# Retention state decayed ahead on GpSimd, and pending conversion work handed out behind the next scores

## Chip, core and metric

The kernel runs on one core of a Trainium2 chip. Its time is the device time of one execution in microseconds (us), the median over several runs. Lower is better. The engines are TensorE (PE; its weight loads are PEld), VectorE (DVE), ScalarE (ACT), GpSimd (POOL) and SyncE (SP, which issues most transfers).

## The reference, cut to what matters

A retention layer feeds two feed-forward layers. There are 2 batches, 8 heads, 768 tokens and a head width of 64; the 1536 token rows have 512 columns.

```python
for t in range(S):                               # retention, per batch and head
    state = gamma * state + outer(k[t], v[t])    # 64 x 64, gamma depends on the head
    y[t] = scale * q[t] @ state
h = x @ w_in;  g = softplus(h);  x = g @ w_out                  # layer 1, d_ff 2048
xn = x / rms(x) * rms_g
out = (silu(xn @ w_gate) * (xn @ w_val)) @ w_out2               # layer 2, d_ff 1536
```

The weights arrive as 64-bit floats; the kernel converts them itself.

## The kernel before, in words

**Tiling.** Retention goes in 12 chunks of 128 tokens (6 per batch; chunk g, place c = g % 6 in its batch). Four chunks make one block of 512 token rows, and there are three blocks. Inside a chunk the recurrence is a matrix product under a causal mask, plus a product with the state carried from the chunk before; one chunk needs these steps:

- `step_t` (L270) turns q and k of a chunk on TensorE (L261). ScalarE copies the turned k (L268), VectorE multiplies the turned q by a table of decays (L263).
- `step_s` (L274) makes the scores of a chunk on TensorE (L280); VectorE multiplies them by two masks (L282), which is what the outputs read.
- `step_y` (L303) makes the outputs on TensorE (L316 from the state, L323 from the masked scores). `split` (L121) takes each of the two halves out of PSUM: ScalarE rounds it to a high part (L122), VectorE subtracts that for a low part (L123). The results are the block's `x`.
- `step_u` (L284) makes the chunk's own contribution `u` to the state on TensorE (L293). VectorE forms the new state as old state times decay plus `u`: a plain copy for c = 0 (L297), four instructions of 64 columns, one per pair of heads, for c = 1 to 4 (L300), nothing for c = 5. The state alternates between two tiles.
- `prep` (L248) scales v on GpSimd (L250).

**Precision.** The large products use three terms: high times high, high times low, low times high. A weight is therefore converted into a high and a low half.

**Conversion of a weight** is in three parts. `convert` (L156) starts it: ScalarE L165 and L166, VectorE L167 and L169, GpSimd L171. It leaves `finish` (L179) in a list of deferred work: VectorE L180. `finish` leaves `last` (L175) there: ScalarE copies the high half (L122) and GpSimd subtracts for the low half (L123). `flush` (L202) runs what is in the list at that moment and then may issue one more weight load on SP (L140). The activation of layer 1 leaves its own split in the same list (`split_later`, L344: ScalarE L122, VectorE L123).

**Order.** The order of instructions is written out by hand: each engine works through its own queue in program order. Chunks 0 to 3 come alone (the loop at L550). Chunks 4 to 11 are each put beside one projection of layer 1, `l1` (L351), 12 matrix products of 512 columns (L340): the loop at L577, with o = 0 to 3 the place in the block and b the block whose layer-1 work runs. There the order of one step is: turn the next chunk, project, then the activation (`after`, L355: ScalarE L357 to L359, VectorE L360), `flush`, outputs, state, next scores, `flush`, `convert`. At chunk 7 the turning of chunk 9 stands between the last scores and the second `flush`. For b = 1, o = 2 and 3, two pieces of layer 1's second product (`l2`, L364, matrix products at L376) follow. Weights are converted in the order `w_in` 0 to 3, then `w_out` 0 to 3: the high half of `w_in` 2 is written in the step of chunk 5, that of `w_in` 3 in chunk 6, `w_out` 0 to 3 in chunks 7 to 10. `l1` of chunk 6 reads `w_in` 2, that of chunk 7 reads `w_in` 3, and the `l2` pieces in the step of chunk 10 read `w_out` 0 to 3. After chunk 11 the rest is layer 1 and layer 2, where TensorE has long runs of products.

The functions around the change:

Of the kernel before, what the change touches and what calls it, by code (L numbers as in the profile page):

```python
# [8 lines left out]
F32 = mybir.dt.float32  # L9
# [3 lines left out]
ALU = mybir.AluOpType  # L13
PSUM = bass.MemoryType.PSUM

P = 128
# [10 lines left out]
def retention_softplus_swiglu(ctx: ExitStack, tc: tile.TileContext, q, k, v, w_in, w_out,  # L27
                              w_gate, w_val, w_out2, rms_g, decay, out):
    nc = tc.nc
    B, H, S, D = q.shape  # L30
# [4 lines left out]
    CPB = S // P  # L35
# [3 lines left out]
    NP = H // 2  # L39
# [3 lines left out]
    const = ctx.enter_context(tc.tile_pool(name="const", bufs=1))  # L43
# [16 lines left out]
    def bank(name):  # L60
        n, s = banks["n"], len(banks["spare"])
        banks["n"] += 1
        if (n + 1) * s // (4 + s) > n * s // (4 + s):
            banks["spare"].append(banks["spare"].pop(0))
            return acc_bank(banks["spare"][-1])
        return ps.tile([P, N], F32, tag="ps", name=name)
# [33 lines left out]
    def load_next(g, weight=False):  # L100
        if g + 1 < NCH:
            load(g + 1, 0)
            load(g + 1, 1)
        if weight:
            load_weight()
        if g < NCH:
            load(g, 2)
# [8 lines left out]
    nc.gpsimd.affine_select(out=causal, in_=causal, pattern=[[1, P]], compare_op=ALU.is_ge,  # L116
                            fill=0.0, base=0, channel_multiplier=-1)
    state = [const.tile([P, NP, D], F32, name=f"state{i}") for i in range(2)]
    nc.scalar.preload_act_table_set("natural_log_exp_and_others")

    def split(hi, lo, src, eng=nc.vector):  # L121
# [18 lines left out]
    def load_weight():  # L140
        i = pos["load"]
        if i >= len(order) or i >= pos["conv"] + STAGE:
            return False
        nm, f = order[i]
        t = stage_p.tile([P, N, 2], U32, tag="stage", name=f"st_{nm}{f}")
        src = srcs[nm]
        if nm in ("w_out", "w_out2"):
            nc.sync.dma_start(out=t, in_=src[f * P:(f + 1) * P])
        else:
            nc.sync.dma_start(out=t.rearrange("p (k f) two -> p k f two", k=KC),  # L150
                              in_=src[:, f * P:(f + 1) * P].rearrange("(k p) f two -> p k f two", p=P))
        staged[i] = t
        pos["load"] += 1
        return True
# [47 lines left out]
    def flush(loads=True):  # L202
        todo = list(deferred)
        deferred.clear()
        for s in todo:
            s()
        if loads:
            load_weight()
# [16 lines left out]
    step = const.tile([P, NP], F32, name="step")  # L225
# [22 lines left out]
    def prep(g):  # L248
        t = qkv[g][2]
        nc.gpsimd.tensor_tensor(out=t, in0=t, in1=dec[:, 1, 0, :, None].to_broadcast([P, H, D]), op=ALU.mult)  # L250
# [19 lines left out]
    def step_t(g, busy=0, order=(1, 0)):  # L270
        turn(g, busy, order)
        turned(g, order)

    def step_s(g):  # L274
        t = tr[g]
        sc = [bank("sc").rearrange("p (j t) -> p j t", j=NP) for _ in range(2)]
        for j in range(NP):
            for e in range(2):
                r = slice(e * D, (e + 1) * D)
                nc.tensor.matmul(sc[e][:, j, :], lhsT=t[r, 1, j, :], rhs=t[r, 0, j, :], start=True, stop=True)  # L280
        for e in range(2):
            nc.vector.tensor_tensor(out=t[:, 2 + e], in0=sc[e], in1=mask[e], op=ALU.mult)  # L282

    def step_u(g):  # L284
        c = g % CPB
        _, kk, vv = [qkv[g].pop(i) for i in range(3)]
        if c == CPB - 1:
            return
        u = bank("u")[:, 0:NP * D].rearrange("p (j t) -> p j t", j=NP)
        for j in range(NP):  # L290
            for e in range(2):
                h = 2 * j + e
                nc.tensor.matmul(u[e * D:(e + 1) * D, j, :], lhsT=kk[:, h, :], rhs=vv[:, NP * e + j, :],  # L293
                                 start=True, stop=True, skip_group_check=True)
        new, old = state[(c + 1) % 2], state[c % 2]
        if c == 0:
            nc.vector.tensor_copy(new, u)  # L297
        else:
            for j in range(NP):
                nc.vector.scalar_tensor_tensor(out=new[:, j], in0=old[:, j], scalar=step[:, j:j + 1], in1=u[:, j],  # L300
                                               op0=ALU.mult, op1=ALU.add)

    def step_y(g):  # L303
        c = g % CPB
# [46 lines left out]
    def l1(b, f):  # L351
        h = bank("h")
        project(h, weight("w_in", f), x[b])

        def after():  # L355
            t = t_p.tile([P, N], F32, tag="t", name="t")
            nc.scalar.activation(out=t, in_=h, func=AF.Abs)  # L357
            nc.scalar.activation(out=t, in_=t, func=AF.Exp, scale=-1.0)
            nc.scalar.activation(out=t, in_=t, func=AF.Ln, bias=1.0)  # L359
            nc.vector.scalar_tensor_tensor(out=t, in0=h, scalar=0.0, in1=t, op0=ALU.max, op1=ALU.add)  # L360
            split_later((b, f), t)
        return after

    def l2(b, gr, m):  # L364
        fs = range(gr * G1, (gr + 1) * G1)
        keep = b == 0
        if keep:
            if gr == 0:
                acc[b, m] = acc_bank(m)
            p = acc[b, m]  # L370
        else:
            p = bank("l2")
        for f in fs:
            w = weight("w_out", f, m == KC - 1)
            for n, (i, j) in enumerate(TERMS):
                nc.tensor.matmul(p, lhsT=w[:, i, m * P:(m + 1) * P], rhs=g_t[b, f][:, j, :],  # L376
                                 start=(n == 0 and f == (0 if keep else fs[0])),
                                 stop=(n == 2 and f == (F1 - 1 if keep else fs[-1])))
        if m == KC - 1:
            for f in fs:  # L380
                g_t.pop((b, f))

        def after():
            if not keep:
                if gr == 0:
                    acc[b, m] = s2_p.tile([P, N], F32, tag="s2", name="x2")
                    nc.scalar.activation(out=acc[b, m], in_=p, func=AF.Copy)
                else:
                    nc.vector.tensor_tensor(out=acc[b, m], in0=p, in1=acc[b, m], op=ALU.add)
            if gr == NG1 - 1:  # L390
                norm(b, m)
        return after
# [134 lines left out]
    def piece(after, conv=1, steps=1):  # L527
        flush()
        for _ in range(conv):
            convert()  # L530
        after()
        if bg:
            step = bg.pop(0)
            if step:
                step()
# [32 lines left out]
    for gr in range(NG1):  # L568
        for b in range(NB):
            l1s = [lambda f=f: l1(b, f) for f in range(gr * G1, (gr + 1) * G1)]  # L570
            if (gr, b) == (NG1 - 1, NB - 1):
                banks["spare"] = list(range(KC))
            l2s = []
            if pend:
                l2s = [lambda m=m: l2(*pend, m) for m in range(KC)]
            if gr == 0 and b < NB - 1:
                for o in range(G1):  # L577
                    g = (b + 1) * CB + o
                    if l2s and o > 1:
                        banks["spare"] = [2, 3] if o == 2 else []  # L580
                    if g + 1 < NCH and g != 2 * CB:
                        step_t(g + 1)
                    after = l1s[o]()
                    if g + 1 < NCH:
                        load_next(g + 2)
                        prep(g + 1)
                    after()
                    flush()
                    step_y(g)
                    step_u(g)  # L590
                    if g + 1 < NCH:
                        step_s(g + 1)
                    if g == 2 * CB - 1:
                        step_t(g + 2)
                    flush()
                    if b == 0 or o < 2:
                        convert()
                    if l2s and o > 1:
                        piece(l2s.pop(0)(), False)
                        piece(l2s.pop(0)(), False)  # L600
            else:
                for n, kind in enumerate("11212122" if (gr, b) == (NG1 - 1, NB - 1) else "12121212"):
                    piece((l1s if kind == "1" else l2s).pop(0)(), n % 2 == 0 and (gr, b) != (NG1 - 1, NB - 1))
            pend = (b, gr)
# [68 lines left out]
```

## Time and profile before

| | us |
|---|---|
| median of 3 timed runs | 627.05 (626.89 to 627.73) |
| profiled execution, span from first to last instruction | 3531.3 |
| PE busy in the profiled execution | 3526.4 |
| DVE, ACT, POOL busy | 360.4, 325.9, 187.2 |

No other time of the profiled execution is given than its span. It lasted 5.63 times as long as the median of the timed runs, and TensorE is busy in nearly all of it. A duration of one instruction is from its start to its written result; when several instructions follow one another on an engine, the distance between their starts (the pitch) is shorter.

### The profile page before, as it was taken

Reading aid. Unit: us, or ns where it says so; the run is one execution under the profiler, and the core shown is the slowest. Engines: PE = TensorE matmul, PEld = TensorE weight load, DVE = VectorE, ACT = ScalarE, POOL = GpSimd, SP = SyncE. Lnnn points to the kernel's source line nnn. Section 1 sums busy time; section 2 is a strip of 40 time slices with the busy share of each in tenths; the row PEclk is TensorE's granted clock in tenths of the full one; section 3 lists DMA queues with packets and bytes.
Section 4 is the critical chain, followed back from the end, with each engine's and each line's share of the span. In section 5 each row is a group of like instructions: output and inputs, shape, how many; then the busy total and the mean of one; then the engine's idle time right before and its main releaser. Section 6 shows DMA issues by size and latency. Waiting matters only on the chain.

```text
span 3531.3 us, 8590 instructions
## 1 busy us (share of the span) xinstructions
PE 3526.4 (100%) x3308; PEld 2460.6 (70%) x3308; DVE 360.4 (10%) x613; ACT 325.9 (9%) x555; POOL 187.2 (5%) x156
## 2 busy tenths in 40 slices
PE   9999999999999999999999999999999999999999
PEld 8777666666666666666776766666666666666666
DVE  1111001101101010011111100000110011100000
ACT  0111011111101010011110010000000000000000
POOL 0001000000000000000000000000000000000000
DMA  3110000000000000000000000000000000000000
GB/s 76 45 33 21 6 12 12 18 18 18 12 0 12 18 18 0 6 18 0 6 18 18 6 18 18 0 12 6 18 18 0 12 10 14 0 0 3 9 6 18
DMA packets 65560, 48.84 MB, mean 14 GB/s; under 512 B 39792, under 2 KB 60528, under 8 KB 65520
## 3 DMA queue, kind: packets, MB, share of 16 engines
q1 hardware_dynamic: 64320, 47.90, 4.6%
q8 instruction: 26, 0.43, 0.0%
q10 hardware_dynamic: 1200, 0.39, 0.0%
q14 instruction: 14, 0.11, 0.0%
HBM read 45.14 MB, written 3.15 MB: 14 GB/s over the span
## 4 chain that ended last, share of the span: by engine, by line
PE 100%; DVE 0%; ACT 0%; issue 0%
PE h L340 19%; PE h_w_val L340 14%; PE h_w_gate L340 14%; PE l L376 12%; PE l L494 10%; PE acc L376 9%; PE acc L494 6%; PE acc L340 6%; PE sc L280 1%; PE y L323 1%; PE pt L261 1%; PE acc L261 1%; PE acc L323 1%; PE acc L280 1%; PE acc L293 1%; PE y L316 0%
## 5 line engine op out<-in xcount | busy, mean ns | idle before, releaser
L340 PE MATMUL h<-x,ws_w_in 128*128 128x512 f32 x516 | 699.5, 1697 | 0.0
L340 PEld LDWEIGHTS h<-x,ws_w_in 128*128 128x128 f32 x516 | 469.4, 911 | 209.0 <-issue 209.0
L340 PE MATMUL h_w_val<-xn,ws_w_val 128*128 128x512 f32 x384 | 519.5, 1693 | 0.0
L340 PE MATMUL h_w_gate<-xn,ws_w_gate 128*128 128x512 f32 x372 | 502.9, 1694 | 0.0
L340 PEld LDWEIGHTS h_w_val<-xn,ws_w_val 128*128 128x128 f32 x384 | 351.1, 916 | 156.0 <-issue 156.0
L340 PEld LDWEIGHTS h_w_gate<-xn,ws_w_gate 128*128 128x128 f32 x372 | 340.1, 914 | 151.8 <-issue 151.4
L376 PE MATMUL l<-g,ws_w_out 128*128 128x512 f32 x324 | 438.4, 1691 | 0.0
L376 PEld LDWEIGHTS l<-g,ws_w_out 128*128 128x128 f32 x324 | 295.3, 912 | 131.7 <-issue 129.2
L494 PE MATMUL l<-ws_w_out,g 128*128 128x512 f32 x261 | 354.6, 1697 | 0.0
L376 PE MATMUL acc<-g,ws_w_out 128*128 128x512 f32 x252 | 340.6, 1699 | 0.0
L494 PEld LDWEIGHTS l<-ws_w_out,g 128*128 128x128 f32 x261 | 236.7, 908 | 106.0 <-issue 104.4
L376 PEld LDWEIGHTS acc<-g,ws_w_out 128*128 128x128 f32 x252 | 229.5, 914 | 102.6 <-issue 100.5
L494 PE MATMUL acc<-ws_w_out,g 128*128 128x512 f32 x171 | 231.1, 1696 | 0.0
L494 PEld LDWEIGHTS acc<-ws_w_out,g 128*128 128x128 f32 x171 | 156.4, 915 | 69.9 <-issue 69.1
L171 POOL TENSOR_TENSOR c<-w,c 128x512 uint32<-128x512 uint32 x68 | 86.0, 1264 | 1635.3 <-DVE w L169 1279.8
L360 DVE SCALAR_TENSOR_TENSOR t<-h,t 128x512 f32<-128x512 f32 x43 | 29.7, 692 | 990.7 <-ACT t L359 990.7
L122 ACT ACTIVATE g<-t 128x512 fp32r<-128x512 f32 x84 | 52.9, 630 | 720.5 <-DVE t L475 686.2
L357 ACT ACTIVATE t<-h 128x512 f32<-128x512 f32 x43 | 25.7, 597 | 1002.7 <-PE h L340 1002.7
L471 ACT ACTIVATE t<-t 128x512 f32<-128x512 f32 x36 | 22.7, 630 | 701.1 <-DVE t L470 701.1
L340 PE MATMUL acc<-x,ws_w_in 128*128 128x512 f32 x60 | 82.6, 1715 | 0.0
L340 PE MATMUL acc<-xn,ws_w_gate 128*128 128x512 f32 x60 | 81.9, 1701 | 0.0
L475 DVE TENSOR_TENSOR t<-h_w_val,t 128x512 f32<-128x512 f32 x32 | 22.1, 691 | 559.3 <-PE h_w_val L340 559.3
(128 smaller groups left out, 1579.8 us busy)
## 6 DMA issues: line engine op xcount, KB each, us to landing
st_w_out<-in_moe_w_out_dram SPq DMA_DIRECT2D x28, 512.0 KB, 3.2
st_w_in<-in_moe_w_in_dram SPq DMA_DIRECT2D x16, 512.0 KB, 3.8
st_w_gate<-in_moe_w_gate_dram SPq DMA_DIRECT2D x12, 512.0 KB, 3.5
st_w_val<-in_moe_w_val_dram SPq DMA_DIRECT2D x12, 512.0 KB, 3.5
v<-in_v_dram SPq DMA_DIRECT2D x12, 256.0 KB, 3.8
q<-in_q_dram SPq DMA_DIRECT2D x23, 128.0 KB, 3.5
k<-in_k_dram SPq DMA_DIRECT2D x23, 128.0 KB, 2.6
out_dram<-o SPq DMA_DIRECT2D x11, 256.0 KB, 2.0
```

The costliest lines, as they stand in the source:

```text
L122: nc.scalar.activation(out=hi, in_=src, func=AF.Copy)
L171: nc.gpsimd.tensor_tensor(out=c, in0=w, in1=c, op=ALU.add)
L261: nc.tensor.transpose(pt[:, j, :], pair(qkv[g][i], j), ident)
L280: nc.tensor.matmul(sc[e][:, j, :], lhsT=t[r, 1, j, :], rhs=t[r, 0, j, :], start=True, stop=True)
L293: nc.tensor.matmul(u[e * D:(e + 1) * D, j, :], lhsT=kk[:, h, :], rhs=vv[:, NP * e + j, :], start=True, stop=True, skip_group_check=True)
L323: nc.tensor.matmul(ys[e][h * D:(h + 1) * D, i, :], lhsT=qkv[g][2][:, NP * e + j, :], rhs=t[:, 2 + e, j, :], start=(c == 0 and i == 0), sto ...
L340: nc.tensor.matmul(h, lhsT=w[:, i, kk * P:(kk + 1) * P], rhs=src[:, j, kk, :], start=(n == 0), stop=(n == 3 * KC - 1))
L357: nc.scalar.activation(out=t, in_=h, func=AF.Abs)
L360: nc.vector.scalar_tensor_tensor(out=t, in0=h, scalar=0.0, in1=t, op0=ALU.max, op1=ALU.add)
L376: nc.tensor.matmul(p, lhsT=w[:, i, m * P:(m + 1) * P], rhs=g_t[b, f][:, j, :], start=(n == 0 and f == (0 if keep else fs[0])), stop=(n == ...
L471: nc.scalar.activation(out=t, in_=t, func=AF.Silu)
L494: nc.tensor.matmul(p, lhsT=g_t[b, f][:, j, m * P:(m + 1) * P], rhs=w[:, i, :], start=(n == 0 and f == (0 if keep else grp[0])), stop=(n == ...
```

## The change

The decayed state is made ahead: after a chunk's state is there, GpSimd multiplies it by the decay into a new tile `faded` (for c = 0 to 3), and the next chunk's state is one VectorE addition of `u` and `faded` over 256 columns instead of four multiply-adds of 64 columns. In the steps of chunks 4 to 11 the first `flush` is moved from ahead of `step_y` to behind `step_s` of the next chunk.

```diff
     state = [const.tile([P, NP, D], F32, name=f"state{i}") for i in range(2)]
+    faded = const.tile([P, NP, D], F32, name="faded")
...
-        new, old = state[(c + 1) % 2], state[c % 2]
+        new = state[(c + 1) % 2]
         if c == 0:
             nc.vector.tensor_copy(new, u)
         else:
-            for j in range(NP):
-                nc.vector.scalar_tensor_tensor(out=new[:, j], in0=old[:, j], scalar=step[:, j:j + 1], in1=u[:, j],
-                                               op0=ALU.mult, op1=ALU.add)
+            nc.vector.tensor_tensor(out=new, in0=u, in1=faded, op=ALU.add)
+        if c < CPB - 2:
+            nc.gpsimd.tensor_tensor(out=faded, in0=new, in1=step[:, :, None].to_broadcast([P, NP, D]), op=ALU.mult)
...
                     after()
-                    flush()
                     step_y(g)
                     step_u(g)
                     if g + 1 < NCH:
                         step_s(g + 1)
+                    flush()
                     if g == 2 * CB - 1:
                         step_t(g + 2)
                     flush()
```

## Rows read from the trace of the kernel before

**Rows 1.** The page: span and busy time of the engines.

```profile
span 3531.3 us, 8590 instructions
PE 3526.4 (100%) x3308; PEld 2460.6 (70%) x3308; DVE 360.4 (10%) x613; ACT 325.9 (9%) x555; POOL 187.2 (5%) x156
```

**Rows 2.** Windows, chunk 4: length, busy PE, PEld, DVE, ACT, POOL, clock, DMA share, GB/s.

```profile
112.89:150.57 37.68, 37.68 (x87) 27.49 (x85) 5.67 (x12) 5.59 (x10) 2.26 (x2) 1.00 0.10 22
```

**Rows 3.** Chain that ended last, the projection of chunk 4: start, length.

```profile
118.26 15.87 PE acc L340 x12
```

**Rows 4.** Timeline of weight loads: first score of chunk 5.

```profile
144.84 0.60 PEld L280 LDWEIGHTS sc<-at 64*128 64x128 f32 x1
```

**Rows 5.** Timeline of ScalarE, chunk 5, and two later rows: start, duration, operation, [idle before].

```profile
171.84 0.60 ACT L357 ACTIVATE t<-acc 128x512 f32<-128x512 f32 x1 [17.83 <-PE acc L340]
174.52 0.63 ACT L122 ACTIVATE g<-t 128x512 fp32r<-128x512 f32 x1 [0.76 <-DVE t L360]
179.90 0.38 ACT L122 ACTIVATE x<-acc 128x256 fp32r<-128x256 f32 x1 [2.17 <-PE acc L323]
180.18 0.62 ACT L122 ACTIVATE ws_w_in<-a 128x512 fp32r<-128x512 f32 x1
180.70 0.66 ACT L165 ACTIVATE c<-st_w_in 128x512 uint32<-128x512 uint32 x1
181.26 0.66 ACT L166 ACTIVATE a<-st_w_in 128x512 f32<-128x512 f32 x1
...
209.44 0.63 ACT L122 ACTIVATE g<-t 128x512 fp32r<-128x512 f32 x1 [0.76 <-DVE t L360]
209.98 0.36 ACT L122 ACTIVATE x<-acc 128x256 fp32r<-128x256 f32 x1
...
260.94 0.60 ACT L268 ACTIVATE at<-pt 128x512 f32<-128x512 f32 x1 [10.80 <-PE pt L261]
261.43 0.62 ACT L122 ACTIVATE ws_w_out<-a 128x512 fp32r<-128x512 f32 x1
```

**Rows 6.** Timeline of VectorE, chunks 4 and 5.

```profile
142.64 0.42 DVE L123 TENSOR_TENSOR x<-acc,x 128x256 fp32r<-128x256 f32 x1 [2.13 <-ACT x L122]
144.96 0.86 DVE L300 SCALAR_TENSOR_TENSOR state<-state,step,u 128x64 f32<-128x64 f32 x4 [1.90 <-PE u L293]
...
173.79 0.69 DVE L360 SCALAR_TENSOR_TENSOR t<-acc,t 128x512 f32<-128x512 f32 x1 [17.13 <-ACT t L359]
174.40 0.68 DVE L180 SCALAR_TENSOR_TENSOR a<-a,c 128x512 f32<-128x512 f32 x1
...
185.60 0.69 DVE L282 TENSOR_TENSOR at<-sc,mask 128x512 f32<-128x512 f32 x1 [4.86 <-PE sc L280]
186.21 0.68 DVE L282 TENSOR_TENSOR at<-acc,mask 128x512 f32<-128x512 f32 x1
186.81 0.42 DVE L167 TENSOR_SCALAR w<-st_w_in 128x512 uint32<-128x512 uint32 x1
187.26 0.69 DVE L169 SCALAR_TENSOR_TENSOR w<-st_w_in,w 128x512 uint32<-128x512 uint32 x1
```

**Rows 7.** Timeline: scaling of v, a weight's low half, and who reads weights first.

```profile
154.39 1.04 POOL L250 TENSOR_TENSOR v<-v,dec 128x512 f32<-128x512 f32 x1
180.88 1.27 POOL L123 TENSOR_TENSOR ws_w_in<-a,ws_w_in 128x512 fp32r<-128x512 f32 x1 [25.45 <-ACT ws_w_in L122]
...
190.08 16.65 PE L340 MATMUL h<-x,ws_w_in 128*128 128x512 f32 x12
...
371.12 32.24 PE L376 MATMUL acc<-g,ws_w_out 128*128 128x512 f32 x24
```

**Rows 8.** Timelines of GpSimd and VectorE later on: two that overlap, and one undisturbed.

```profile
796.62 1.51 POOL L123 TENSOR_TENSOR ws_w_in<-a,ws_w_in 128x512 fp32r<-128x512 f32 x1 [28.27 <-ACT ws_w_in L122]
...
701.81 0.69 DVE L169 SCALAR_TENSOR_TENSOR w<-st_w_in,w 128x512 uint32<-128x512 uint32 x1
...
797.04 1.65 DVE L169 SCALAR_TENSOR_TENSOR w<-st_w_in,w 128x512 uint32<-128x512 uint32 x1
```

## The prediction

> **What bounds the kernel now.** I read the page first [rows 1]. TensorE is busy in 3526.4 of 3531.3 us, VectorE in 360.4, ScalarE in 325.9. But the profiled execution lasted 3531.3 / 627.05 = 5.63 times the median of the timed runs, and nothing but its span is given of what lay around it. So TensorE's durations can't hold in the timed runs: its busy time alone is over five times their length. Those of the other engines can: 360.4 and 325.9 us fit into 627. In the profile everything hides behind a TensorE that is far too slow; the argument has to be made at the timed pace. I take the rows of VectorE, ScalarE and GpSimd as they stand and multiply TensorE's by 627.05 / 3531.3 = 0.178. That is a mean, and an upper one, as the 627.05 also hold waits; the other bound is the row as it stands, where nothing ever waits on another engine and the change is worth nothing.
>
> Next the window of chunk 4 [rows 2]: one retention step beside one projection takes TensorE 37.68 us, at the timed pace 6.69. VectorE is busy 5.67 in it and ScalarE 5.59, so beside a fast TensorE all three are nearly full, and the order of each queue decides who waits. The projection has 15.87 of the 37.68 [rows 3], 2.82 at the timed pace; outputs and state, from its end at 134.13 to the first score at 144.84 [rows 4], 10.71 or 1.90; scores and turning have the rest, 1.97. So from the end of one projection TensorE comes to the next after 1.90 + 1.97 = 3.87 us.
>
> **ScalarE's and VectorE's queues, before.** Count from the start of the activation's first part, just behind the projection. Pitches are taken from ScalarE's rows [rows 5] and VectorE's [rows 6]. VectorE's part of the activation starts at 173.79 - 171.84 = 1.95 us, the split's ScalarE copy at 174.52 - 171.84 = 2.68. Then ScalarE has the two output copies at +0.54 (209.98 - 209.44) and +0.28, taking for the one between two output copies that from an output copy to the weight's copy, 180.18 - 179.90; the weight's high copy starts another 0.28 later, at 3.78, and with 0.62 is done at 4.40. It has waited for nothing: `finish` stood on VectorE right behind the activation. The next projection, for o = 2 and 3, reads that very weight [rows 5, 7]: TensorE is there at 3.87 and waits 0.5 us. Eight of its twelve products need the high half (1.9 us), so the low half, 1.27 us on GpSimd [rows 7], is in time.
>
> **After, part one: the first flush behind the scores.** It removes nothing and adds no instruction. On SP it passes no other transfer: the loads of q, k and v stand ahead of it in both versions, so the weight load keeps its place; on GpSimd `last` keeps its place too. But on VectorE `finish` now stands behind both output splits, the state and both masks, and both flushes run one after the other, so ScalarE meets `last`, which waits for `finish`, at once. VectorE at a pitch of 0.61 for 512 columns (174.40 - 173.79), 0.60 between masks, and 0.34 for 256 columns (0.42 less the 0.08 by which the larger ones' pitch is under their duration) [rows 6]: activation 1.95, splits 2.56 and 2.90, state 3.24, masks 3.58 and 4.18, `finish` 4.78 to 5.46. The weight's copy starts at 5.50 and is done at 6.12, against 4.40. What the move brings forward are the outputs' splits and the masks. Before, VectorE had the activation's split at 175.18 - 171.84 = 3.34, then splits 3.95 and 4.29, state 4.63, masks 5.49 and 6.09 to 6.78; the next outputs begin on TensorE at 6.69, with products that read no mask, so they hardly waited. I take nothing for it.
>
> Twice (`w_in` 2 and 3) a projection on TensorE stands directly behind this copy: 2 x (6.12 - 4.40) = **+3.4 us**. Nothing covers it, as all of TensorE's work up to there is counted in the 3.87.
>
> Behind the waiting copy stand, on ScalarE, the next conversion's two parts (at 6.02 and 6.57), the copy of the next turned k (about 7.1) and the next activation (7.1 + 0.49 = 7.6) [rows 5]. So ScalarE and VectorE form a loop of 7.6 us per step, where TensorE needs 6.69. In the steps of chunks 7, 8 and 9 no projection waits for a weight, and the lateness adds up: 7.1 - 6.7 = 0.4 (at chunk 7 the k copy stands ahead), 0.9, 0.9, together 2.2. In chunk 10's step the `l2` pieces read `w_out` 3 at once [rows 7]: the low half is there at 6.12 + 0.06 + 1.27 + 2.2 = 9.65, before at 4.40 + 0.06 + 1.27 = 5.73, when TensorE came to it with hardly a wait. **+3.9 us**.
>
> **Part two: the state.** Four instructions of 64 columns took 0.86 [rows 6]; one of 256 columns with one input from PSUM takes 0.42 (the split's row [rows 6]). That saves 0.44 in 8 chunks, 3.5 us of VectorE. In steps 4 to 11 it is inside the loop counted above. Chunks 1 to 3 stand alone: VectorE has there two splits 0.7, state 0.86, masks 1.2, turned q 0.6 and a conversion's 1.7, some 5.0 us against TensorE's 3.87, so I take it in full: 3 x 0.44 = **-1.3 us** (bounds 0 and -1.3).
>
> GpSimd's new product of 256 columns has no row. It lies between 0.52, half of v's scaling over 512 columns, and 1.27, the subtraction over 512 [rows 7]; I take 0.55, nearest to the scaling, which is the same operation with a spread factor. GpSimd's step is then 1.04 + 1.26 + 1.27 + 0.55 = 4.1 of 6.7 us, and the result is needed a chunk later: nothing on the path. It waits for the state (about 3.6); behind it in GpSimd's queue stands the weight's low half, which waits for ScalarE until 6.18 anyway. Without that cover it would cost 8 x 0.55 = 4.4.
>
> Two engines can also be in each other's way. While GpSimd subtracted at 796.62, a VectorE instruction with two SBUF inputs took 1.65 us instead of 0.69, and GpSimd's own 1.51 instead of 1.27 [rows 7, 8]. The Trainium skill, "SBUF — State Buffer", section "SBUF: two separate sides", has the rule: the two share a port pair as an exclusive lock, and whoever comes second is blocked for the whole instruction; the trace agrees. By it alone, each new GpSimd product could hold VectorE for its length and the change would be a loss of its own. I take zero: the product starts right after the state, when VectorE does the masks, which have one input from PSUM; no row here shows a mask beside a GpSimd instruction, so this is an argument only. The late weight subtraction (6.2 to 7.5) now meets the next conversion on VectorE, up to 0.96 in six steps; TensorE needs that VectorE work only at about 8.6. Zero, with 5.8 as the end for the range.
>
> **Sum.** 627.05 + 3.4 + 3.9 - 1.3 = 633.05: **633.0 us**.
>
> **Rivals.**
> *VectorE is the bound (faster).* If TensorE's retention work is so short, or the transfers so late, that VectorE sets the pace of all steps, and the weights' copies are not what TensorE waits for, the 8 x 0.44 = 3.5 us come through: 623.5. For it: VectorE's 5.67 of 6.69. Against: the loop of 7.6 is longer than VectorE's own work. It decides where TensorE comes to a projection later than 6.12.
> *TensorE covers all (no change).* If outputs, state, scores and turning take over 6.1 us at the timed pace and not 3.87, the copy is never late: 627 to 627.5. For it: the rows as they stand; the scaling is a mean over two kinds of product, and small ones may scale worse.
> *The lock (slower for another reason).* Eight products of 0.55 blocking VectorE, less the 3.5 saved: a net 0.9, and with the larger clash of 0.96 in six steps up to 5.8 more: 628 to 634. The rule named above would give this. Against it: the masks have one SBUF input.
>
> **Chances.** Forecast 0.50 (629 to 638), lock 0.07, no change 0.20, faster 0.23 (622 to 626). A difference under 0.2%, 1.25 us, can't be told from none. So slower 0.57, same 0.20, faster 0.23. The range reaches from 624.5, which takes in about half of the faster case, to 638, the forecast's upper end with most of the clash; the likeliest case's own range is 629 to 638.
>
> **What would show it.** In the profile of the changed kernel ScalarE's `ws_w_in` and `ws_w_out` copies in chunks 5 to 10 should stand behind an idle stretch that VectorE's L180 ends, and L180 should follow the second mask; if TensorE is as slow there as now, they will, with no cost visible. A VectorE state instruction should take about 0.42, the GpSimd product about 0.55, and the masks should stay at 0.69. The prediction is wrong if the time falls: then the copy is not on TensorE's path, and the price of TensorE's small products is the step to blame.

## The result, and the profile after

| | us |
|---|---|
| changed kernel, median of 4 runs | 634.12 (634.06 to 635.76) |
| kernel before, beside it, median of 4 runs | 626.97 (626.88 to 627.73) |
| ratio | 1.0118, 95% interval 1.0106 to 1.0130 |

The change costs 7.15 us. The profile of before that stands ahead of the prediction is of an execution whose TensorE was over five times too slow, so the kernel before was profiled once more, unchanged, as the first experiment: 626.85 us, span 624.9, TensorE busy for 615.0 of it. "Before" below is that execution (its lines have the numbers used above); the lines of the changed kernel are one higher (L341 for L340, L181 for L180).

The page of the changed kernel: span, busy time, and two groups of matrix products (busy time, mean ns of one | idle before).

```profile
span 632.5 us, 8577 instructions
PE 617.5 (98%) x3308; PEld 511.2 (81%) x3308; DVE 385.4 (61%) x589; ACT 322.2 (51%) x555; POOL 198.7 (31%) x164
...
L341 PE MATMUL h<-x,ws_w_in 128*128 128x512 f32 x516 | 126.0, 394 | 4.7 <-ACT ws_w_in L123 4.7
...
L377 PE MATMUL acc<-g,ws_w_out 128*128 128x512 f32 x252 | 62.4, 398 | 2.1 <-ACT ws_w_out L123 1.5
```

The same lines of before.

```profile
span 624.9 us, 8590 instructions
PE 615.0 (98%) x3308; PEld 510.1 (82%) x3308; DVE 386.7 (62%) x613; ACT 322.0 (52%) x555; POOL 193.3 (31%) x156
...
L340 PE MATMUL h<-x,ws_w_in 128*128 128x512 f32 x516 | 124.5, 390 | 1.6 <-ACT ws_w_in L122 1.6
...
L376 PE MATMUL acc<-g,ws_w_out 128*128 128x512 f32 x252 | 60.8, 391 | 0.5 <-POOL ws_w_out L123 0.5
```

Two things are to be seen. TensorE waits 4.7 us, not 1.6, for the high half of `w_in`, and 2.1, not 0.5, for `w_out`. And the same 516 and 252 products take 1.5 and 1.6 us longer, though none was added. The first is the mechanism of the forecast, the second was not in it.

The wait on its three engines: the timeline of the changed kernel, VectorE's rows of the step of chunk 5, then ScalarE's and TensorE's of this step and the next.

```profile
40.57 0.41 DVE L124 TENSOR_TENSOR x<-acc,x 128x256 fp32r<-128x256 f32 x1
40.91 0.68 DVE L283 TENSOR_TENSOR at<-sc,mask 128x512 f32<-128x512 f32 x1
41.50 0.68 DVE L283 TENSOR_TENSOR at<-acc,mask 128x512 f32<-128x512 f32 x1
42.10 0.68 DVE L181 SCALAR_TENSOR_TENSOR a<-a,c 128x512 f32<-128x512 f32 x1
...
37.68 0.60 ACT L358 ACTIVATE t<-acc 128x512 f32<-128x512 f32 x1 [1.58 <-PE acc L341]
...
42.81 0.63 ACT L123 ACTIVATE ws_w_in<-a 128x512 fp32r<-128x512 f32 x1 [1.82 <-DVE a L181]
...
52.02 0.63 ACT L123 ACTIVATE ws_w_in<-a 128x512 fp32r<-128x512 f32 x1 [2.15 <-DVE a L181]
...
43.50 3.02 PE L341 MATMUL h<-x,ws_w_in 128*128 128x512 f32 x12 [2.12 <-ACT ws_w_in L123]
...
52.70 4.57 PE L341 MATMUL h<-x,ws_w_in 128*128 128x512 f32 x12 [2.58 <-ACT ws_w_in L123]
```

The same copies and projections of before.

```profile
41.85 0.63 ACT L122 ACTIVATE ws_w_in<-a 128x512 fp32r<-128x512 f32 x1 [0.59 <-DVE a L180]
...
49.33 0.63 ACT L122 ACTIVATE ws_w_in<-a 128x512 fp32r<-128x512 f32 x1
...
42.53 3.02 PE L340 MATMUL h<-x,ws_w_in 128*128 128x512 f32 x12 [0.76 <-ACT ws_w_in L122]
...
50.01 3.04 PE L340 MATMUL h<-x,ws_w_in 128*128 128x512 f32 x12 [0.86 <-ACT ws_w_in L122]
```

`finish` (L181) now stands behind both masks, ScalarE stands idle 1.82 and 2.15 us for it, and TensorE 2.12 and 2.58. The second of these projections then takes 4.57 us instead of 3.04.

Windows of 1 us over that projection in the changed kernel: length, busy PE, PEld, DVE, ACT, POOL, granted clock, DMA share, GB/s.

```profile
52.00:53.00 1.00, 0.30 (x1) 0.30 (x2) 0.97 (x3) 0.98 (x2) 0.28 (x1) 0.81 0.90 171
53.00:54.00 1.00, 1.00 (x3) 0.81 (x3) 1.00 (x1) 1.00 (x3) 1.00 (x1) 0.50 0.99 214
...
56.00:57.00 1.00, 1.00 (x6) 0.70 (x4) 0.00 (x0) 0.00 (x0) 1.00 (x2) 0.98 0.77 283
```

The granted clock falls from 1.00 to 0.50, that is from 2.4 to 1.2 GHz, at the end of the wait of 2.58 us. It is 0.50 in the three windows from 53 to 56, and 0.98 in the one from 56. The second place is the last weight of `l2`. TensorE's timeline there in the changed kernel, and a window over the second row, with the fields as above:

```profile
85.78 0.73 PE L377 MATMUL acc<-g,ws_w_out 128*128 128x512 f32 x2 [1.52 <-ACT ws_w_out L123]
87.13 4.65 PE L377 MATMUL acc<-g,ws_w_out 128*128 128x512 f32 x13 [0.62 <-POOL ws_w_out L124]
...
88.00:89.00 1.00, 1.00 (x3) 0.71 (x3) 0.00 (x0) 0.00 (x0) 0.00 (x0) 0.50 0.00 0
```

And before:

```profile
80.99 3.24 PE L376 MATMUL acc<-g,ws_w_out 128*128 128x512 f32 x13 [0.50 <-POOL ws_w_out L123]
```

Thirteen products take 4.65 us behind the waits of 1.52 and 0.62, with the clock at 0.50 again, and 3.24 behind one of 0.50.

ScalarE's first rows of the activations of chunks 7 to 10 in the changed kernel:

```profile
57.30 0.60 ACT L358 ACTIVATE t<-h 128x512 f32<-128x512 f32 x1 [3.04 <-PE h L341]
64.43 0.58 ACT L358 ACTIVATE t<-h 128x512 f32<-128x512 f32 x1
72.02 0.59 ACT L358 ACTIVATE t<-h 128x512 f32<-128x512 f32 x1
79.64 0.59 ACT L358 ACTIVATE t<-acc 128x512 f32<-128x512 f32 x1
```

Those of chunks 7 and 10 before.

```profile
53.09 0.60 ACT L357 ACTIVATE t<-h 128x512 f32<-128x512 f32 x1 [1.51 <-PE h L340]
...
74.40 0.60 ACT L357 ACTIVATE t<-acc 128x512 f32<-128x512 f32 x1 [0.48 <-PE acc L340]
```

**The account**, along the activations and TensorE, spans 632.5 - 624.9 = 7.6 us:

| stretch | after | before | difference |
|---|---|---|---|
| to the first projection | 27.68 | 27.39 | +0.29 |
| from there to the activation of chunk 7 | 29.62 | 25.70 | +3.92 |
| from there to that of chunk 10 | 22.34 | 21.31 | +1.03 |
| from there to the low half of the last `w_out` | 7.49 | 6.59 | +0.90 |
| the 13 products behind it | 4.65 | 3.24 | +1.41 |

The sum is 7.55; what follows is equal. The +3.92 are 3.08 more of waiting for weights and 4.57 - 3.02 = 1.55 of half clock, less 0.61 that before waits for a turned q (TensorE's first scores at 39.59) and after does not, and a rest of -0.1.

### The profile page after: what moved, and what is told of

It reads as the page before. It is cut to its first block, busy times and chain, and to the rows that moved or that the text cites. A ratio compares the mean times of both kernels' runs of the same rounds, so it can differ in the third digit from the quotient of the medians.

```text
span 632.5 us, 8577 instructions
## 1 busy us (share of the span) xinstructions
PE 617.5 (98%) x3308; PEld 511.2 (81%) x3308; DVE 385.4 (61%) x589; ACT 322.2 (51%) x555; POOL 198.7 (31%) x164
## 4 chain that ended last, share of the span: by engine, by line
PE 89%; DVE 3%; ACT 3%; DMA 2%; SPq 1%; issue 1%; POOL 0%; POOLq 0%
PE h L341 18%; PE h_w_val L341 14%; PE h_w_gate L341 13%; PE l L377 12%; PE l L495 9%; PE acc L377 9%; PE acc L495 6%; PE acc L341 6%; DVE at L283 1%; DMA k<-in_k_dram 1%; DMA v<-in_v_dram 1%; DVE x L124 1%; DMA q<-in_q_dram 1%; ACT t L359 1%; ACT t L360 1%; DVE t L361 1%
## 5 line engine op out<-in xcount | busy, mean ns | idle before, releaser
L341 PE MATMUL h<-x,ws_w_in 128*128 128x512 f32 x516 | 126.0, 394 | 4.7 <-ACT ws_w_in L123 4.7
L341 PEld LDWEIGHTS h<-x,ws_w_in 128*128 128x128 f32 x516 | 97.7, 190 | 25.5 <-ACT ws_w_in L123 5.2
L341 PE MATMUL h_w_val<-xn,ws_w_val 128*128 128x512 f32 x384 | 92.3, 389 | 0.0
L341 PE MATMUL h_w_gate<-xn,ws_w_gate 128*128 128x512 f32 x372 | 89.4, 389 | 0.0
L341 PEld LDWEIGHTS h_w_val<-xn,ws_w_val 128*128 128x128 f32 x384 | 72.0, 188 | 14.9
L341 PEld LDWEIGHTS h_w_gate<-xn,ws_w_gate 128*128 128x128 f32 x372 | 69.8, 188 | 14.5
L377 PE MATMUL l<-g,ws_w_out 128*128 128x512 f32 x324 | 78.0, 389 | 0.0
L377 PEld LDWEIGHTS l<-g,ws_w_out 128*128 128x128 f32 x324 | 60.7, 188 | 12.6
L377 PE MATMUL acc<-g,ws_w_out 128*128 128x512 f32 x252 | 62.4, 398 | 2.1 <-ACT ws_w_out L123 1.5
L495 PE MATMUL l<-ws_w_out,g 128*128 128x512 f32 x261 | 63.0, 390 | 0.0
L181 DVE SCALAR_TENSOR_TENSOR a<-a,c 128x512 f32<-128x512 f32 x68 | 58.1, 855 | 3.7 <-POOL c L172 3.7
```

What stands on the lines that cost most here:

```text
L181: nc.vector.scalar_tensor_tensor(out=a, in0=a, scalar=TINY, in1=c.bitcast(F32), op0=ALU.is_ge, op1=ALU.mult)
L341: nc.tensor.matmul(h, lhsT=w[:, i, kk * P:(kk + 1) * P], rhs=src[:, j, kk, :], start=(n == 0), stop=(n == 3 * KC - 1))
L495: nc.tensor.matmul(p, lhsT=g_t[b, f][:, j, m * P:(m + 1) * P], rhs=w[:, i, :], start=(n == 0 and f == (0 if keep else grp[0])), stop=(n == ...
```

## The experiments

All ratios are to the kernel before, run beside each kernel on the same chip (626.84 to 626.99), with 95% intervals.

**The kernel before, unchanged**, for a profile at the pace of the timed runs.

> The kernel before, unchanged, for a profile at the timed pace. Theory (late finish): 627; in the steps of chunks 5 and 6 the weight's high copy on ScalarE follows the output copies with no wait, TensorE waits for it at most 0.9 us each time instead of 2.1 and 2.6, a step lasts 6.9 to 7.0 us throughout, and the half-clock stretches of the changed kernel (52.7 to 56.8 and behind the wait of chunk 10) are absent. If TensorE waits as long in the kernel before, the theory falls.

626.85 us; 0.9998 (0.9988 to 1.0008). It shows what the profile ahead of the prediction could not: VectorE and GpSimd are already in each other's way. Timelines of GpSimd and VectorE, steps of chunks 9 and 5:

```profile
70.05 1.04 POOL L250 TENSOR_TENSOR v<-v,dec 128x512 f32<-128x512 f32 x1
...
70.12 1.52 DVE L180 SCALAR_TENSOR_TENSOR a<-a,c 128x512 f32<-128x512 f32 x1 [0.25 <-POOL c L171]
...
40.30 1.52 DVE L180 SCALAR_TENSOR_TENSOR a<-a,c 128x512 f32<-128x512 f32 x1 [0.25 <-POOL c L171]
```

`finish` waits for GpSimd's product `c` (L171), and as that ends, GpSimd goes on to the scaling of v and holds VectorE's `finish` for 1.52 us instead of 0.68. So it is in the steps of chunks 5, 8 and 10 too: L180 starts at 62.87, 70.12 and 77.40 in those of chunks 8 to 10, a loop of 7.25 and 7.28 us.

**The state alone.**

```diff
-            for j in range(NP):
-                nc.vector.scalar_tensor_tensor(out=new[:, j], in0=old[:, j], scalar=step[:, j:j + 1], in1=u[:, j],
-                                               op0=ALU.mult, op1=ALU.add)
+            nc.vector.tensor_tensor(out=new, in0=u, in1=faded, op=ALU.add)
+        if c < CPB - 2:
+            nc.gpsimd.tensor_tensor(out=faded, in0=new, in1=step[:, :, None].to_broadcast([P, NP, D]), op=ALU.mult)
```

> The state's part alone, the first flush where it was. Theory (late finish): no wait is added, and the first 27 us are set by transfers, so the 0.44 us saved per chunk are worth nothing there: 626 to 627.3, ratio 0.999 to 1.001. Rival (GpSimd's new product blocks VectorE, or is late): 630 or more, with masks or other VectorE rows lengthened beside the product.

627.70 us; 1.0013 (1.0004 to 1.0021), 0.4 above what was expected: no gain, if anything a loss. Up to the first projection TensorE waits for transfers of k (1.7 us), for the scaling of v (0.4) and once for ScalarE (0.2), never for VectorE. So VectorE's saving in chunks 1 to 3 frees nothing: in chunks 1 and 2 the 0.43 us end in a new idle stretch of 0.37 ahead of the masks, which wait for their scores. Later the product stands in GpSimd's queue ahead of a weight that TensorE waits for. Timelines of VectorE (a mask of chunk 2), GpSimd and TensorE in this kernel:

```profile
22.76 0.69 DVE L283 TENSOR_TENSOR at<-sc,mask 128x512 f32<-128x512 f32 x1 [0.37 <-PE acc L281]
...
51.02 0.61 POOL L302 TENSOR_TENSOR faded<-state,step 128x256 f32<-128x256 f32 x1 [3.00 <-DVE state L298]
51.59 1.27 POOL L124 TENSOR_TENSOR ws_w_in<-a,ws_w_in 128x512 fp32r<-128x512 f32 x1
...
50.27 2.11 PE L341 MATMUL h<-x,ws_w_in 128*128 128x512 f32 x8 [0.86 <-ACT ws_w_in L123]
52.92 1.19 PE L341 MATMUL h<-x,ws_w_in 128*128 128x512 f32 x4 [0.54 <-POOL ws_w_in L124]
```

The high half is there at 49.59 + 0.63 = 50.22 (ScalarE's row); the low half could start then, but GpSimd first waits for the state and starts it at 51.59. TensorE runs the eight products of the high half and stands still 0.54 us.

**The move alone.**

```diff
                     after()
-                    flush()
                     step_y(g)
                     step_u(g)
                     if g + 1 < NCH:
                         step_s(g + 1)
+                    flush()
```

> The moved flush alone, the state as before. Theory (late finish): the whole loss is here and a little more, since four state instructions stand in the loop with 0.86 instead of 0.42: five steps of 0.44 more, 634 to 637. Rival (the GpSimd product costs the time): 627.

637.01 us; 1.0163 (1.0149 to 1.0177). The whole loss, and 2.9 us more, is in the move. TensorE's rows:

```profile
43.48 4.61 PE L340 MATMUL h<-x,ws_w_in 128*128 128x512 f32 x12 [2.12 <-ACT ws_w_in L122]
54.28 4.43 PE L340 MATMUL h<-x,ws_w_in 128*128 128x512 f32 x12 [2.58 <-ACT ws_w_in L122]
...
90.36 3.25 PE L376 MATMUL acc<-g,ws_w_out 128*128 128x512 f32 x13 [0.62 <-POOL ws_w_out L123]
```

The waits are those of the changed kernel. With the old state in the loop the activations of chunks 8 to 10 start at 66.31, 74.36 and 82.44, steps of 8.05 and 8.08 where the changed kernel has 7.59 and 7.62: the four small instructions cost 0.46 each time once `finish` stands behind them. So the state's part saves some 2 to 3 us here, and nothing alone.

**`finish` back ahead of the outputs, the split of the activation left behind the scores.**

```diff
                     after()
+                    mine = deferred.pop()
+                    flush(False)
+                    deferred.insert(0, mine)
                     step_y(g)
```

(on the changed kernel)

> As the changed kernel, but the weight's finish is handed out ahead of the outputs again, and only the activation's split and the weight's last part stay behind the scores. Theory (late finish): ScalarE meets last with finish long done, the loop is open, no half-clock stretch: 625 to 627.5, so 7 us or more under the changed kernel. Rival (anything else behind the moved flush, or the GpSimd product): 632 to 634 stays.

626.60 us; 0.9996 (0.9987 to 1.0005). One deferred step put back takes the loss away: TensorE waits 1.2 us for `w_in`'s high halves, and the clock is 1.00 throughout. It gains nothing over before; `finish` meets GpSimd's scaling of v again (1.51 us at 63.31, 70.88 and 78.48).

**The waits filled with small products**, to keep TensorE busy: `keep_busy(8)` ahead of the two projections and ahead of the last weight of the first `l2` piece.

```diff
+                    if b == 0 and o > 1:
+                        keep_busy(8)
                     after = l1s[o]()
...
+            if (b, gr, m, f) == (0, 0, 0, fs[-1]):
+                keep_busy(8)
```

> The changed kernel with eight small products of ones (L214's kind) on TensorE in each of the three waits (ahead of the projections of chunks 6 and 7, and ahead of the fourth weight of the first l2 piece), some 1.7 us of otherwise idle time. Theory (the idle wait costs a half-clock stretch on top): granted clock stays 1.0 through 43 to 58 and behind 87 us, time 634.1 less about 3.0 = 630.5 to 632. Rival (the half clock has another cause, or costs nothing in the end): 634 or more.

633.53 us; 1.0103 (1.0089 to 1.0117), a miss: more was expected to come back. Both projections do take 3.02 and 3.06, and from the activation of chunk 4 to that of chunk 7 it is 24.32 us instead of 26.13. But each call takes a PSUM tile and shifts all that follow: TensorE's wait of 2.51 us for a mask at 74.95 is new, and the projection behind it takes 4.47. So this run can't tell the clock's part from that of the shifted tiles; the next one leaves the tiles as they are:

**The same products written into the projection's own tile**, for the two projections alone.

```diff
         h = bank("h")
+        if (b, f) in ((0, 2), (0, 3)):
+            for _ in range(8):
+                nc.tensor.matmul(h[:, 0:P], lhsT=ones, rhs=ones, start=True, stop=True)
         project(h, weight("w_in", f), x[b])
```

> The changed kernel, with eight fp32 products of 128 columns on ones written into the projection's own PSUM tile just ahead of the projections of chunks 6 and 7, the two that wait longest for a weight; the first projection product overwrites them. No tile is taken for it, so no other order changes. Theory, the half clock is a cost of its own behind these two waits: the granted clock stays at 1.00 there, both projections take 3.0 to 3.1 us instead of 3.02 and 4.57, the stretch from chunk 4's activation to chunk 7's shrinks by 1.3 to 1.8 from 26.13, and the time is 632.2 to 632.9 (from 634.1). Rival, what the earlier filled version gained in that stretch was no clock effect but came from its shifted tiles: both projections stay as they were and the time is 634 or more.

631.27 us (631.24 to 631.66); 1.0070 (1.0056 to 1.0084): 2.85 us less than the changed kernel, more than expected. TensorE's timeline: the small products, the two projections, and the last weight of `l2`.

```profile
41.25 1.95 PE L356 MATMUL h<-ones 128*128 128x128 f32 x16
43.54 3.01 PE L341 MATMUL h<-x,ws_w_in 128*128 128x512 f32 x12 [0.34 <-ACT ws_w_in L123]
49.99 1.95 PE L356 MATMUL h<-ones 128*128 128x128 f32 x16
52.74 3.01 PE L341 MATMUL h<-x,ws_w_in 128*128 128x512 f32 x12 [0.80 <-ACT ws_w_in L123]
...
84.31 0.73 PE L380 MATMUL acc<-g,ws_w_out 128*128 128x512 f32 x2 [1.53 <-ACT ws_w_out L123]
85.66 3.24 PE L380 MATMUL acc<-g,ws_w_out 128*128 128x512 f32 x13 [0.62 <-POOL ws_w_out L124]
```

The projections start when they did (43.54 for 43.50, 52.74 for 52.70), so the weights are as late as ever; but the second takes 3.01, not 4.57, and the stretch from chunk 4's activation to chunk 7's is 24.43 instead of 26.13. The 13 products at the end also take 3.24 instead of 4.65, though nothing was put there and the waits ahead of them are the same. The activation of chunk 7 starts at 55.79 for 57.30, 1.51 earlier, and the 13 products save 1.41: 2.9 of the 3.0 between the spans (632.5 and 629.5). The half clock is shown as a cost of its own, about 3 us of the 7.6; the late weights, the loop and 0.3 at the start are the other 4.6.

**Where `flush` may stand.** Three kernels with the first `flush` in other places: behind `step_u`, with the new state; behind `step_y`, with the old state; behind `step_y`, with the new state.

The first:

```diff
                     after()
-                    flush()
                     step_y(g)
                     step_u(g)
+                    flush()
                     if g + 1 < NCH:
                         step_s(g + 1)
```

The second and third:

```diff
                     after()
-                    flush()
                     step_y(g)
+                    flush()
                     step_u(g)
```

> As the changed kernel, but the first flush between the state and the next scores, so finish and the activation's split stand ahead of the masks and behind output splits and state. Theory (what costs is finish behind the masks): the weight's copy is done about 4.9 us after the activation's start instead of 6.1, steps of 6.95 us as TensorE needs, 625.5 to 627.5. Rival (any place behind the outputs costs): 630 or more.

626.46 us; 0.9993 (0.9984 to 1.0002).

> The kernel before with the first flush between the outputs and the state. Theory (loops): finish is no longer held by the scaling of v on GpSimd (1.52 instead of 0.68 us in three steps of the kernel before), the weight's copy is done about 4.2 us after the activation's start, steps fall from 7.25 to 6.95: 625 to 626.5. Rival (those 0.84 us were hidden): 626.9, no change.

625.61 us (625.27 to 626.26); 0.9979 (0.9971 to 0.9988).

> The same place of the flush with the new state (GpSimd product). Theory (loops): 625 to 627, within 0.8 us of the version with the old state, the difference being the start of the first projection (27.7 to 28.2 us with the GpSimd product, 27.4 without, so far). Rival (the new state helps once the flush is out of the way): 0.5 us or more under the version with the old state.

625.97 us; 0.9986 (0.9978 to 0.9995).

It is the masks that may not stand ahead of `finish`: with the `flush` only those two instructions earlier the 7 us are gone, and the clock stays at 1.00. Behind the outputs alone it beats both kernels, by 1.2 us against before. TensorE's waits in that kernel (engine, line, waited for: us, times, longest) and VectorE's `finish`:

```profile
PE h L340 <- ACT ws_w_in L122: 1.8, 2, 1.1
PE acc L261 <- DMA k<-in_k_dram: 0.7, 1, 0.7
...
70.92 0.68 DVE L180 SCALAR_TENSOR_TENSOR a<-a,c 128x512 f32<-128x512 f32 x1
```

With two splits ahead of `finish`, GpSimd's scaling of v is over when it comes, or nearly (0.92 at 63.95, 0.68 at 70.92, for 1.52 before), and the steps of chunks 8 to 10 are 6.96 to 6.97 us, with ScalarE waiting for TensorE's projection in them. The old state is ahead of the new one by 0.36 us, too little for these intervals to tell, but of the same sign as in the run with the state alone.

## Why the prediction was right, and where its steps were not

The forecast was 633.0, the time 634.12, and the likeliest case is the one that came. Its steps:

**The first flush behind the scores: +3.4.** Right in its mechanism, some 1.0 too large. The copy is done 42.81 + 0.63 - 37.68 = 5.76 and 6.10 us after the activation's start, forecast 6.12. Before, it is done 41.85 + 0.63 - 37.39 = 5.09 and 4.37 after it, forecast 4.40: in the first of the two steps it was late already, as `finish` was held there by GpSimd's scaling of v (1.52 us at 40.30). TensorE waits 3.08 us more for the two weights, and 0.61 less for a turned q, which the move brings forward and for which nothing was taken: net 2.47.

**The loop of ScalarE and VectorE: +3.9.** The half about the changed kernel held to the tenth: steps of 7.13, 7.59 and 7.62 us, forecast 7.1, 7.6 and 7.6; the low half of the last `w_out` read 7.49 us after chunk 10's activation, forecast 6.12 + 0.06 + 1.27 = 7.45. It came to 1.03 + 0.90 = +1.93, because the half about the kernel before was mis-sized: "TensorE needs 6.69" is 6.96, 6.97 and 7.38 in its three steps (21.31, not 20.07), and the low half is read 6.59 us after the activation, not 5.73. Two things lie in that. The 6.69 was a mean scale put on TensorE's rows; its own pace is 6.96 to 6.97, which the kernel with the `flush` behind the outputs keeps in all three steps: some 0.8 of the 1.24. The other 0.4, and the late low half, come with `finish` held by GpSimd's scaling of v; the kernel that frees it has neither. In the profile ahead of the prediction these two instructions never met.

**The state: -1.3.** Wrong. The one addition takes 0.41 us as forecast, but TensorE never waits for VectorE in chunks 1 to 3; the first projection starts at 27.68, before at 27.39. The step that failed is "some 5.0 us against TensorE's 3.87, so I take it in full": TensorE's work was compared without its waits for transfers there, and the forecast's own lower bound, 0, was the value. That start varies from 27.2 to 28.35 among the ten kernels profiled, with no order by what was changed; why was not tried.

**GpSimd's product: 0.55, off the path.** It takes 0.61 to 0.62 in six of eight cases, and 0.80 and 1.06 in chunks 1 and 3, where it meets VectorE's conversion work (L168, L181). In the changed kernel nothing waits for it; with the `flush` in its old place it delays a weight's low half (0.54 us), since the cover named, a low half that waits for ScalarE anyway, is there only with the move.

**The clash of GpSimd and VectorE: taken at 0.** Right in its price, though not because they never meet: beside the products of chunks 1 and 2, L170 at 19.99 took 0.98 us and `finish` at 23.62 took 0.90, before 0.69 and 0.68. TensorE waits for neither. The timelines of the step of chunk 6:

```profile
50.33 0.61 POOL L302 TENSOR_TENSOR faded<-state,step 128x256 f32<-128x256 f32 x1 [2.48 <-DVE state L298]
52.72 1.34 POOL L124 TENSOR_TENSOR ws_w_in<-a,ws_w_in 128x512 fp32r<-128x512 f32 x1 [1.78 <-ACT ws_w_in L123]
...
50.11 0.68 DVE L283 TENSOR_TENSOR at<-sc,mask 128x512 f32<-128x512 f32 x1
50.71 0.68 DVE L283 TENSOR_TENSOR at<-acc,mask 128x512 f32<-128x512 f32 x1
...
52.96 1.66 DVE L170 SCALAR_TENSOR_TENSOR w<-st_w_out,w 128x512 uint32<-128x512 uint32 x1
```

The masks, with one input in PSUM, keep their 0.68 beside the product; the argument for which there was no row holds. The conversion's L170, with both inputs in SBUF, is held for 1.66 by the low half's subtraction, as [rows 8] had it; but VectorE stands idle 4.04 us ahead of its next activation (its row at 59.26), so it costs nothing. The lock rival's price did not come; where that lock does cost is in the kernel before, whose VectorE and GpSimd go round in 7.25 us.

**Not in the sum: TensorE's clock, +3.0.** The forecast priced the waits, not what follows them. With it taken out by the filled waits the measured loss is 631.27 - 626.99 = 4.28, where the steps gave 6.0. So the closeness of 633.0 to 634.12 is partly luck. Against the account, 1.0 too much for the two copies and 2.0 too much in the loop stand against a gain of 1.3 that did not come, a start 0.3 later, and 3.0 of clock: 7.6 where the steps gave 6.0. No row ahead of the prediction could show the clock's part, as TensorE hardly ever waited in that profile.

## What to carry to other kernels

Deferred work has a due time at its far end: before a `flush` is moved, list what stands between its old and new place on each engine that carries the chain to the next matrix product; here two masks on VectorE cost 7 us, while two splits in the same place gain 1.2. Saved instructions pay only on the engine that sets the pace of that stretch: the same state change was worth some 2 to 3 us behind the moved `flush` and nothing without it. And a profile whose span is not near the timed runs gives durations, but not which instructions meet, nor the pace of the kernel that a loop is compared with.

## What the runs showed of the hardware that was not expected

A wait of TensorE can cost more than its length. At the end of a wait of 2.58 us the granted clock fell to 0.50 (1.2 GHz) and a projection took 4.57 us instead of 3.02; behind one of 2.12 it did so with the move alone (4.61) and not in the changed kernel (3.02); behind the one of 2.51 in the first filled kernel it did so as well (4.47). Behind the waits of 1.52 and 0.62 at `l2` it fell in the changed kernel (4.65 for 3.24), but not behind the same waits with the earlier ones filled (3.24), nor behind 1.96 and 0.62 with the move alone (3.25). So the length of the last wait alone does not decide; what does was not settled here.

The Trainium skill, "SBUF — State Buffer", section "SBUF: two separate sides", has GpSimd and VectorE lock each other out of shared ports. For VectorE instructions with two SBUF inputs, which the section names, the runs agree: one went from 0.68 to 1.52 beside a GpSimd product of 1.04. One with a PSUM input stayed at 0.68 beside a product of 0.61.
